# Two engines share the last three output evictions of a sorted-attention and token-mixing kernel

## The chip, the cores and the metric

The kernel runs on one core of a Trainium2 chip. The core has a matrix engine (TensorE, PE in the profile), three engines for elementwise work (VectorE or DVE, ScalarE or ACT, GpSimd or POOL) and SyncE (SP), which here only issues DMA transfers. TensorE writes its results to PSUM, a memory of eight banks; one row of 512 f32 numbers on each of 128 partitions fills one bank. ScalarE and VectorE read PSUM and write SBUF, the working memory, from which DMA takes the output to the chip's main memory (HBM). The metric is the device time of one execution in microseconds (us), of which the median over several runs is compared. A profile is one execution, and its span runs from the first to the last instruction.

## What is computed

Two layers, one behind the other, for 4 batches of 768 positions. The first is attention within blocks of 96 positions, with keys and values mixed over the 8 blocks by a small matrix that is normalised five times. The second mixes positions with weights worked out from the result itself:

```python
# x: the attention's result, (4, 768, 512)
wq = x @ w_q                                   # 512 -> 64
wk = x @ w_k
W_tok = scale * np.einsum('bsd,btd->bst', wq, wk)
mixed = np.einsum('bst,btd->bsd', W_tok, x)
return (np.maximum(mixed, 0.0) @ w_out).astype(np.float32)
```

The change concerns how the last product, `... @ w_out`, leaves the core.

## The kernel before

Everything is tiled by batch (b = 0 to 3), and the stages of neighbouring batches overlap. The order of the work on all engines is written out by hand: ORDER (lines 18 to 48) is a list of short items, each a call of one small function. In an item the first letter is the stage, then come batch and part, then an engine (A ScalarE, D VectorE, G GpSimd, S SyncE) and a PSUM bank. A capital letter is mostly TensorE's work into a bank, and the small letter of the same stage takes the result out of that bank (an eviction). So `O33:0` computes part 3 of the output of batch 3 into bank 0, and `o33:A:0` copies bank 0 to SBUF on ScalarE. Each engine executes its own items in the order of the list. The waits between engines are not written by hand: the tile framework in which the kernel is written puts them in from what each instruction reads and writes.

The positions of a batch are dealt out as 768 = 128 x 6: partition p holds positions 6p to 6p+5, and "row" r of 0 to 5 is the one with remainder r. The last stages of a batch are these:

- H and h (lines 407 to 421): the mixed result, transposed, for two rows at a time, and its relu, which is the eviction to `mixT`. Each call uses two banks. In batch 3 h32 is on VectorE and h30 and h31 are on ScalarE.
- O and o (lines 423 to 432): four accumulating matmuls of 128x512 for each row into one bank, and the copy of that bank into one half of an `ot` tile, which holds two rows in f32. There are four `ot` tiles, used in turn.
- s (lines 434 to 440): the store of a row from `ot` to HBM, issued on SP. In batch 3 each row is a store of its own, 256 KB.

The list ends with batch 3: its rows are computed in the order 5, 4, 0, 3, 2, 1, with the evictions D, A, D, A, A, A. The last three go out of banks 0, 7 and 4, and no later matmul writes these. All eight banks are one tile, `PS` (line 100); `copy` (lines 146 to 150) is `nc.scalar.copy` for the letter A and `nc.vector.tensor_copy` for any other, so that all such copies carry line 148 or 150 in the profile. After the list come a check on GpSimd (lines 443 to 455) of reciprocals that were stored on the way, and a branch to a slow general computation that is not taken here.

Of the kernel before, what the change touches and what calls it, by code (L numbers as in the profile page):

```python
# [42 lines left out]
O12:0 o15:A:3 D30:S H20:6 o12:D:0 H22:2 H21:4 h20:A:6 O13:1 h21:D:4 O20:0 h22:D:2 O23:7 o20:A:0 o13:A:1 J31:2  # L43
o23:D:7 s11:S J30:0 s12:S j31:D:2 O22:7 j30:D:0 d31:D d30:A W31:0 W30:2 o22:A:7 O21:1 w30:D:2 w31:A:0 s21:S
G30:0 o21:D:1 G31:0 s20:S O25:7 g30:A:0 H32:0 o25:A:7 H30:2 H31:4 h32:D:0 h30:A:2 O24:6 O35:0 o24:A:6 h31:A:4
s22:S O34:7 o35:D:0 O30:4 s35:S o34:A:7 O33:0 s34:S o30:D:4 O32:7 s30:S o33:A:0 O31:4 s33:S o32:A:7 s32:S
o31:A:4 s31:S
"""


# [1 line left out]
def kernel(  # L52
# [12 lines left out]
    B, H, S, D = q.shape  # L65
# [9 lines left out]
    DM = moe_w_out.shape[0]  # L75
# [24 lines left out]
    PS = psp.tile([P, 8, 512], FP32, name="ps")  # L100
# [45 lines left out]
    def copy(e, o, i):  # L146
        if e == "A":
            nc.scalar.copy(o, i)  # L148
        else:
            nc.vector.tensor_copy(o, i)  # L150
# [277 lines left out]
    def oslot(b, n):  # L428
        return ot[(b * 3 + n // 2) % NOT]

    def u_o(b, n, e, bank):
        copy(e, oslot(b, n)[:, n % 2, :], PS[:, bank, :])

    def u_s(b, n, e, bank):
        od = out[b].rearrange("(p r) e -> p r e", r=R6)
# [173 lines left out]
    for item in ORDER.split():  # L609
# [5 lines left out]
        b, n = int(name[1]), int(name[2:])  # L615
# [41 lines left out]
```

## Time and profile before

| | us |
|---|---|
| runs before: 99.10, 98.98, 98.49; median | 98.98 |
| profiled execution, its own time | 99.35 |
| span of the profiled execution | 97.5 |
| granted TensorE clock, as a share of full speed | 1.00 |

The page of the profile has the busy time of each engine, the span in 40 slices, the chain of work that ended last (followed back from the last instruction, at each step to what released it) and the costliest groups of instructions. Other views answer questions on the same execution: the chain in order of time, the instructions in order of time, groups with each shape of operand kept apart, who waited for whom, and the DMA transfers. In a row of a group stand the line, the engine, the operation, output and input with their shapes, the count, then busy time in us and the mean of one in ns, and after the next bar the idle time ahead of it with what ended it. In a row of the timeline stand start and duration in us, and in square brackets the idle time before it and what ended it.

### The profile page before, as it was taken

How to read it: one execution, taken by the hardware profiler on the slowest of the kernel's cores; microseconds unless marked ns; L12 is line 12 of the kernel's file. 1: busy time of each engine (PE TensorE's matmuls, PEld its weight loads, DVE VectorE, ACT ScalarE, POOL GpSimd, SP SyncE). 2: the span in 40 equal slices, each digit the busy share in tenths (PEclk: the TensorE clock that was granted, in tenths of full speed). 3: DMA queues.
4: the chain of work that ended last, by engine and by line, in shares of the span. 5: the costliest groups of instructions: out<-in, count | busy, mean ns of one | idle time of the engine just before them, and what ended most of it. 6: DMA issues, size and time to landing. Idle time of an engine off the chain costs nothing.

```text
span 97.5 us, 3326 instructions
## 1 busy us (share of the span) xinstructions
PE 85.6 (88%) x1396; PEld 58.8 (60%) x1406; DVE 66.4 (68%) x133; ACT 70.7 (73%) x102; POOL 30.9 (32%) x50
## 2 busy tenths in 40 slices
PE   4994978959989998989999999999899999999950
PEld 1333567847878576747875687985676555654410
DVE  2677985848995457879876569986596897535300
ACT  5411199987878999979789999899968644549450
POOL 5994009999405860000000077000300380000000
PEclk9999999999999999999999999999999999999999
DMA  0799999999999999999999999889999993691973
GB/s 3 69 199 203 203 205 207 201 203 204 205 217 210 224 246 221 203 206 202 213 248 249 226 198 232 135 176 92 265 424 328 86 245 148 260 383 72 403 309 133
DMA packets 26144, 20.62 MB, mean 211 GB/s; under 512 B 8336, under 2 KB 23440, under 8 KB 26128
## 3 DMA queue, kind: packets, MB, share of 16 engines
q0 software_dynamic: 14064, 10.09, 68.6%
q1 hardware_dynamic: 12064, 10.31, 40.1%
q8 instruction: 11, 0.18, 0.7%
q14 instruction: 5, 0.04, 0.1%
HBM read 20.19 MB, written 6.29 MB: 272 GB/s over the span
## 4 chain that ended last, share of the span: by engine, by line
PE 45%; DMA 32%; POOL 8%; ACT 4%; issue 3%; SPq 2%; DVE 1%; ACTq 0%; DVEq 0%; POOLq 0%
PE ps L144 45%; DMA Vn<-in_v_dram 21%; DMA Qn<-in_q_dram 8%; POOL M L240 5%; DMA VT<-Vs 4%; POOL wqk L209 2%; ACT KT L148 2%; SPq L366 1%; DVE mixT L421 1%; ACT Vs L148 1%; ACT QT L148 1%; POOL Kn L216 1%; POOL wo L211 1%; SPq L302 1%; ACT ot L148 1%
## 5 line engine op out<-in xcount | busy, mean ns | idle before, releaser
L316 ACT ACTIVATE E<-ps 96x960 bf16<-96x960 f32 (+1 forms) x28 | 24.1, 897 | 2.1 <-PE ps L144 1.9
L144 PE MATMUL ps<-wo,mixT 128*128 128x512 bf16 x87 | 22.2, 379 | 0.9 <-issue 0.3
L345 DVE TENSOR_TENSOR X<-ps,Rall 96x896 bf16<-96x896 f32 (+1 forms) x20 | 20.0, 1005 | 0.6
L144 PEld LDWEIGHTS <-mixT 128*128 128x128 bf16 x96 | 8.3, 97 | 9.2 <-issue 0.8
L148 ACT COPY ot<-ps 128x512 f32<-128x512 f32 x17 | 9.9, 586 | 4.8 <-PE ps L144 4.3
L144 PE MATMUL ps<-VT,E 96*128 96x65 bf16 x256 | 10.9, 193 | 0.9 <-DMA VT<-Vs 0.3
L144 PEld LDWEIGHTS <-E 96*128 96x128 bf16 x256 | 9.5, 97 | 3.1 <-issue 2.0
L382 POOL COPY qD<-qkT 64x384 bf16<-64x384 bf16 x4 | 1.9, 500 | 29.1 <-ACT qkT L148 20.0
L148 ACT CAST KT<-ps 128x768 bf16<-128x768 f32 x12 | 9.3, 804 | 1.4 <-PE ps L144 1.0
L240 POOL TENSOR_TENSOR M<-PTR,m_p 128x512 bf16<-128x512 bf16 x6 | 7.8, 1314 | 7.2 <-ACT KT L148 6.1
L144 PEld LDWEIGHTS <-KT 64*128 64x128 bf16 (+1 forms) x288 | 8.3, 97 | 2.7 <-issue 1.2
L150 DVE CAST KT<-ps 128x768 bf16<-128x768 f32 x8 | 7.6, 955 | 2.2 <-PE ps L144 2.1
L144 PE MATMUL ps<-QT,KT 64*128 64x96 bf16 x256 | 9.0, 204 | 0.0
L419 ACT ACTIVATE mixT<-ps 128x1024 bf16<-128x1024 f32 x8 | 8.2, 1025 | 0.6 <-PE ps L144 0.6
L144 PE MATMUL ps<-fil 128*128 128x512 bf16 x21 | 7.4, 526 | 1.4 <-DVE fil L192 1.2
L144 PE MATMUL ps<-M,Kn 128*64 128x128 bf16 x192 | 7.5, 220 | 1.2 <-DMA Kn<-in_k_dram 0.4
L150 DVE COPY ot<-ps 128x512 f32<-128x512 f32 x7 | 4.8, 690 | 4.1 <-PE ps L144 3.8
L144 PEld LDWEIGHTS <-Kn 128*64 128x64 bf16 x192 | 6.4, 109 | 1.9 <-issue 0.8
L148 ACT CAST Vs<-ps 128x1024 bf16<-128x1024 f32 x7 | 6.9, 1017 | 0.8 <-PE ps L144 0.7
L144 PE MATMUL ps<-Vn,M 128*128 128x128 bf16 x72 | 5.5, 219 | 1.5 <-DMA Vn<-in_v_dram 1.3
L421 DVE TENSOR_SCALAR mixT<-ps 128x1024 bf16<-128x1024 f32 x4 | 4.8, 1222 | 2.3 <-PE ps L144 2.2
L340 DVE RECIPROCAL Rall<-ps 96x14 f32<-96x14 f32 (+1 forms) x20 | 4.4, 224 | 2.7 <-PE ps L144 2.7
(80 smaller groups left out, 130.3 us busy)
## 6 DMA issues: line engine op xcount, KB each, us to landing
out_dram<-ot SPq DMA_DIRECT2D x18, 256.0 KB, 2.2
Qn<-in_q_dram POOLq DMA_DIRECT2D x4, 768.0 KB, 22.8
Vn<-in_v_dram POOLq DMA_DIRECT2D x4, 768.0 KB, 18.4
Kn<-in_k_dram POOLq DMA_DIRECT2D x4, 768.0 KB, 17.0
VT<-Vs SPq DMA_DIRECT2D x18, 132.0 KB, 6.4
out_dram<-ot SPq DMA_DIRECT2D x3, 512.0 KB, 4.1
wo<-in_moe_w_out_dram POOLq DMA_DIRECT2D x1, 512.0 KB, 17.0
wqk<-in_moe_w_q_dram POOLq DMA_DIRECT2D x1, 64.0 KB, 14.7
```

What stands on the lines that cost most here:

```text
L144: nc.tensor.matmul(o, w, x, is_transpose=t, start=start, stop=stop, skip_group_check=True)
L148: nc.scalar.copy(o, i)
L150: nc.vector.tensor_copy(o, i)
L209: nc.gpsimd.dma_start(out=wqk[:, :, s, :], in_=w.rearrange("(t p) d -> p t d", p=P))
L211: nc.gpsimd.dma_start(out=wo, in_=moe_w_out.rearrange("(t p) d -> p t d", p=P))
L240: ENG[e].tensor_tensor(out=M[b % 2][:, h0:h0 + hn], in0=src.unsqueeze(2).to_broadcast([P, hn, SP, NB]), in1=m_p.unsqueeze(1).unsqueeze(3). ...
L316: nc.scalar.activation(E[b % 2][:, n, 0:2 * w * BLK].rearrange("p (t a c) -> p a t c", a=2, c=BLK), PS[0:BLK, bank:bank + 2, 0:w * BLK].re ...
L340: nc.vector.reciprocal(Rall[:, b, n, :, 0:w], avps(bank, w)[:, :, :, D])
L345: nc.vector.tensor_mul(xo.rearrange("p (a t d) -> p a t d", a=2, d=D), avps(bank, w)[:, :, :, 0:D], Rall[:, b, n, :, 0:w].unsqueeze(3).to_ ...
L382: nc.gpsimd.tensor_copy(o, i)
L419: nc.scalar.activation(o, i, ACT.Relu)
L421: nc.vector.tensor_relu(o, i)
```

## The change

An item of stage o may now name two engines. The row is then cut into as many pieces of columns as there are letters, and each engine copies its piece: with `AD`, ScalarE columns 0 to 255 and VectorE columns 256 to 511 of the same bank, into the same `ot` tile. The last three evictions of the list, rows 3, 2 and 1 of batch 3, become `AD`; all other items keep one letter and one copy of 512 columns. The matmuls, the banks and the stores stay as they are.

```diff
-s22:S O34:7 o35:D:0 O30:4 s35:S o34:A:7 O33:0 s34:S o30:D:4 O32:7 s30:S o33:A:0 O31:4 s33:S o32:A:7 s32:S
-o31:A:4 s31:S
+s22:S O34:7 o35:D:0 O30:4 s35:S o34:A:7 O33:0 s34:S o30:D:4 O32:7 s30:S o33:AD:0 O31:4 s33:S o32:AD:7 s32:S
+o31:AD:4 s31:S
...
     def u_o(b, n, e, bank):
-        copy(e, oslot(b, n)[:, n % 2, :], PS[:, bank, :])
+        o, w = oslot(b, n)[:, n % 2, :], DM // len(e)
+        for i, x in enumerate(e):
+            copy(x, o[:, i * w:(i + 1) * w], PS[:, bank, i * w:(i + 1) * w])
```

## The prediction

> **What bounds the kernel now.** The page comes first, for the busy shares and for the chain of work that ended last.
>
> ```profile
> span 97.5 us, 3326 instructions
> PE 85.6 (88%) x1396; PEld 58.8 (60%) x1406; DVE 66.4 (68%) x133; ACT 70.7 (73%) x102; POOL 30.9 (32%) x50
> PE 45%; DMA 32%; POOL 8%; ACT 4%; issue 3%; SPq 2%; DVE 1%; ACTq 0%; DVEq 0%; POOLq 0%
> ```
>
> TensorE carries 45% of the chain and loads of the inputs 32%; evictions are a few per cent. But the edit touches three evictions at the very end, so what counts is the last stage. There I read the chain in order of time.
>
> ```profile
> 87.33 1.24 DVE mixT L421
> 88.56 0.05 issue
> 88.61 5.37 PE ps L144 x24
> 93.98 0.02 issue
> 94.00 0.59 ACT ot L148
> ```
>
> From 88.61 on TensorE computes the last six output rows, 24 matmuls without a gap: 5.37/6 = 0.895 us a row at most (the first matmuls overlap the row before). The chain leaves it only when it has finished, and then runs through one eviction, that of row 1. The timeline of the last evictions shows that this is the only one of the six whose length can be seen at the end:
>
> ```profile
> 91.47 0.69 DVE L150 COPY ot<-ps 128x512 f32<-128x512 f32 x1 [1.09 <-PE ps L144]
> 92.27 0.59 ACT L148 COPY ot<-ps 128x512 f32<-128x512 f32 x1 [1.10 <-PE ps L144]
> 93.14 0.59 ACT L148 COPY ot<-ps 128x512 f32<-128x512 f32 x1 [0.28 <-PE ps L144]
> 94.00 0.59 ACT L148 COPY ot<-ps 128x512 f32<-128x512 f32 x1 [0.28 <-PE ps L144]
> ```
>
> These are rows 0, 3, 2 and 1, in that order. ScalarE starts a row every 0.87 us, works 0.59 and then waits 0.28 for TensorE: it is no bottleneck, and VectorE has nothing to do after 91.47 + 0.69 = 92.16. What follows the evictions is SP's queue and the closing of the program:
>
> ```profile
> 92.88 0.33 SPq L440 DMA_DIRECT2D out_dram<-ot  x1
> 93.75 0.33 SPq L440 DMA_DIRECT2D out_dram<-ot  x1
> 94.61 0.33 SPq L440 DMA_DIRECT2D out_dram<-ot  x1
> out_dram<-ot SPq DMA_DIRECT2D x4, 256.0 KB, 2.0
> ```
>
> Each store is issued 0.02 us after its eviction (94.00 + 0.59 = 94.59, issue at 94.61) and lands 2.0 us later (the last line, from the DMA view of 92 us to the end): 96.6. The 0.9 us from there to 97.5 are the barrier at the end. So the last 97.5 - 94.59 = 2.9 us hang rigidly on the end of the last eviction, and the question is when row 1 is out of PSUM.
>
> **The change, part by part.** Three ScalarE copies of 128x512 become three of 128x256, and VectorE gets three of 128x256. The other rows carry one letter, so their width stays DM/1 = 512 and nothing of them moves. The costs come from the groups of instructions with shapes kept apart:
>
> ```profile
> L148 ACT COPY ot<-ps 128x512 f32<-128x512 f32 x17 | 9.9, 586 | 4.8 <-PE ps L144 4.3 <-ACT mixT L419 0.4
> L150 DVE COPY ot<-ps 128x512 f32<-128x512 f32 x7 | 4.8, 690 | 4.1 <-PE ps L144 3.8 <-ACT ot L148 0.3
> L403 ACT ACTIVATE Ab<-ps 128x256 bf16<-128x256 f32 x3 | 1.2, 384 | 1.7 <-PE ps L144 1.7
> L405 DVE TENSOR_SCALAR Ab<-ps 128x256 bf16<-128x256 f32 x1 | 0.4, 416 | 0.0
> L148 ACT COPY wk<-ps 96x256 bf16<-96x256 bf16 x5 | 1.9, 377 | 0.6 <-PE ps L144 0.6
> L150 DVE CAST PTR<-ps 128x256 bf16<-128x256 f32 x1 | 0.4, 414 | 0.0
> ```
>
> No row is the half copy itself (256 columns of f32 out of PSUM into f32), but two of each engine have its length: 0.377 and 0.384 us on ScalarE, 0.414 and 0.416 on VectorE. I take 0.384 and 0.416. Half the columns cost 66% of 0.586 and 60% of 0.690: much of a copy is a fixed part, which is now paid on both engines.
>
> What the trace does not show is how the two halves stand to each other. They lie in one PSUM bank, since a row is the whole of PS[:, bank, :]. In the kernel before, every bank is read by one engine at a time. What it shows is this pair from the timeline, both engines at once:
>
> ```profile
> 87.33 1.23 DVE L421 TENSOR_SCALAR mixT<-ps 128x1024 bf16<-128x1024 f32 x1 [1.69 <-PE ps L144]
> 87.47 1.02 ACT L419 ACTIVATE mixT<-ps 128x1024 bf16<-128x1024 f32 x1
> ```
>
> They read different banks of the one tile PS (0 and 1, 2 and 3) and write different columns of the one tile mixT, side by side. So neither the tile that is read nor the one that is written forces an order; whether a bank does is open. This gives two ends. If the halves run side by side, the slower one counts: 0.416 - 0.586 = -0.170 us, a gain. If VectorE's half has to wait for ScalarE's, both count and the handover between them, for which the nearest rows are an exponential on ScalarE and the reduction on VectorE that waits for it:
>
> ```profile
> 2.81 0.26 ACT L160 ACTIVATE Pm<-Pm 32x64 f32<-32x64 f32 x1 [0.79 <-DVE Pm L172]
> 3.10 0.21 DVE L174 TENSOR_REDUCE tmp<-Pm 32x8 f32<-32x64 f32 x1 [0.32 <-ACT Pm L160]
> ```
>
> The handover is 3.10 - (2.81 + 0.26) = 0.03 us. Then 0.384 + 0.03 + 0.416 - 0.586 = +0.244 us, a loss. I take the serial end. The pair above is concurrent because its banks differ; apart from it every bank in this program passes whole from one engine to the next, with a wait between, and two engines in one bank would be something that this kernel never does. Since waits are put in by the program's dependency tracking and not by hand, a tracker that knows the banks adds this one by itself.
>
> [...]
>
> Now the rest of the path. Row 3: ScalarE 92.27 to 92.65, VectorE 92.68 to 93.10. Row 2: 93.14 to 93.52, then 93.55 to 93.97. Row 1: 94.00 to 94.38, then 94.41 to 94.83, where it was 94.59. VectorE is free at 92.16, 93.10 and 93.97, ahead of each of its halves. Behind its waits stand only its next halves and the drain at its end, so nobody else waits. ScalarE gets freer. TensorE isn't touched: no later row goes into the three banks. If those covers were gone (VectorE's half of row 2 running past 94.41), each 0.1 us would be added to the end one for one.
>
> SP's three stores now wait for two engines. Extra waits appear in the trace as instructions of their own:
>
> ```profile
> L440 SPq EVENT_SEMAPHORE  x13: 17/17/17, 69.4 to 94.1; - x13
> L150 DVEq EVENT_SEMAPHORE  x21: 21/21/2557, 16.1 to 89.7; - x21
> ```
>
> One costs 17 ns on SP (minimum, median and maximum agree) and 21 ns at least on VectorE. ScalarE's half is done 0.45 us before VectorE's, so SP passes that wait early, and VectorE passes TensorE's while ScalarE still reads: both at nothing. In the other order they cost 0.02 each, 0.04 in all. Each of the three stores is issued 0.24 us later, their distance stays 0.87, and their landing stays 2.0 us. SP's queue holds nothing else behind them. VectorE's closing drain moves from 92.16 to 94.83, still before the landing at 96.6 plus 0.24.
>
> Sum: +0.24 us, with ends of 0.377 + 0.03 + 0.414 - 0.586 = +0.235 and 0.244 + 0.04 = +0.28 if serial, and -0.17 if side by side. The profiled execution took 99.35 us, 1.85 more than its span, and would become 99.59. The median of the three runs shown is 98.98 (98.49 to 99.10), 0.37 below the profiled one; on it the forecast is 99.22.
>
> **The rivals.** First, the halves run side by side: the end moves to 94.00 + 0.416 = 94.42, and the median to 98.81. For it speaks that VectorE is idle from 92.16, that the two engines do work at once at 87.5 us, and that the written columns are disjoint. Against it, that no row shows one bank read twice. The point that decides is whether VectorE's copy starts within some 0.05 us of ScalarE's or at its end.
>
> Second, clearly slower: VectorE has to fetch code for instructions that it didn't have. It gets three copies and a few waits, and its list could run over into a further block, fetched only when it is reached. The nearest prices are these, from the DMA view of the whole run:
>
> ```profile
> q14 instruction: 5, 0.04, 0.1%
> Pm<-in_sort_net_dram SPq DMA_DIRECT2D x1, 8.0 KB, 1.6
> ```
>
> Five code packets hold 0.04 MB, 8 KB each, and a transfer of 8 KB took 1.6 us to land. If it stood ahead of the last half it would give 0.24 + 1.6 = 1.84, a median of 100.82. Against it: the chain above has no such wait anywhere near the end (issue is 0.02 us there), so blocks seem to be fetched ahead. It decides only if the boundary falls within the last six instructions or so.
>
> Third, the change doesn't do what it says at the end: a fixed part of the split copy is smaller or larger than in my rows, so that the two orders cancel and nothing is left. For no change the serial pair would have to take 0.586, 0.28 each with the handover; no row of 256 columns above is under 0.377, so this has almost no chance.
>
> **How the numbers follow.** Serial 0.78, side by side 0.13, a code fetch or another stall of over 1 us 0.08, none of these 0.01. The likeliest gives 99.22. For the range, the profiled execution shows that one execution can lie 0.37 above the median; 99.35 + 0.28 = 99.63, so the high end is 99.7. At the low end serial on the fastest run is 98.49 + 0.235 = 98.73, and side by side on the median is 98.81; half of the latter's lower spread (0.17 below the fastest run would be 98.32) takes the low end to 98.5. What is left out is the stall and the low corner of the second case, under 2 in 10.
>
> About 1%, 0.99 us, is what a measurement of this kernel can tell from no change. Serial and side by side both lie within it by a wide margin. Faster by over 1% would need more than the whole eviction of 0.586 to vanish: 0.02, for drift alone. Slower by over 1% holds the stall and drift: 0.10. Within 1%: 0.88.
>
> **What would show it.** In the timeline of the end, six copies of 128x256 stand in place of three of 128x512. Right: VectorE's half of each of the three rows starts about 0.03 us after ScalarE's ends, about 0.41 after it started; the last ends 0.83 us after TensorE's end instead of 0.59; the last store is issued 0.02 us behind it; the time from there to the end of the span stays 2.9 us. The chain's last pieces would be ACT ot 0.38 and DVE ot 0.42. Wrong: halves that start together (the rival, 0.17 less), half copies off 0.38 or 0.42 us (the sizes), a VectorE copy slower than its rows because of ScalarE beside it, a gap before VectorE's copy with both engines done (the code), or a landing of the last store that isn't 2.0 us.

## The result and the profile after

The changed kernel takes 99.34 us (median of 16 runs, 99.24 to 99.85), the kernel before 98.94 (16 runs, 98.49 to 99.17). The ratio is 1.0054, with a 95% interval of 1.0041 to 1.0067: 0.4 to 0.7 us slower. The ratio is worked out from all runs; the two medians alone lie 0.40 us apart, at the low end of it. The forecast was 99.22 us, +0.24.

The profiled execution of the changed kernel took 99.34 us. Two lines of its page, and the last pieces of its chain of waits in order of time (start, length, what):

```profile
span 97.2 us, 3331 instructions
PE 85.7 (88%) x1396; PEld 58.8 (61%) x1406; DVE 67.8 (70%) x136; ACT 70.1 (72%) x102; POOL 30.9 (32%) x50
```

```profile
87.98 5.37 PE ps L144 x24
93.35 0.02 issue
93.37 0.38 ACT ot L148
93.75 0.02 issue
93.77 0.42 DVE ot L150
```

The six rows take TensorE 5.37 us, as before. Behind them the chain now goes through two copies with a gap of 0.02 us between: 0.02 + 0.38 + 0.02 + 0.42 = 0.84 us from TensorE's end to the end of the last copy, where it was 0.02 + 0.59 = 0.61. The timeline of the changed kernel shows the same for all three rows (start, length, in brackets the idle time before and what ended it):

```profile
91.64 0.37 ACT L148 COPY ot<-ps 128x256 f32<-128x256 f32 x1 [1.10 <-PE ps L144]
92.05 0.42 DVE L150 COPY ot<-ps 128x256 f32<-128x256 f32 x1 [0.52 <-ACT ot L148]
92.51 0.37 ACT L148 COPY ot<-ps 128x256 f32<-128x256 f32 x1 [0.49 <-PE ps L144]
92.91 0.42 DVE L150 COPY ot<-ps 128x256 f32<-128x256 f32 x1 [0.44 <-ACT ot L148]
93.37 0.37 ACT L148 COPY ot<-ps 128x256 f32<-128x256 f32 x1 [0.49 <-PE ps L144]
93.77 0.42 DVE L150 COPY ot<-ps 128x256 f32<-128x256 f32 x1 [0.44 <-ACT ot L148]
```

VectorE's idle time ahead of each half ends with ScalarE, never with TensorE. The two engines don't share the row, they take turns. The groups with shapes apart give the means, 373 and 424 ns:

```profile
L150 DVE COPY ot<-ps 128x256 f32<-128x256 f32 x3 | 1.3, 424 | 1.4 <-ACT ot L148 1.4
L148 ACT COPY ot<-ps 128x256 f32<-128x256 f32 x3 | 1.1, 373 | 2.1 <-PE ps L144 2.1
```

The last store and the landing of the last four, from SP's timeline and the DMA view:

```profile
94.23 0.33 SPq L442 DMA_DIRECT2D out_dram<-ot  x1
out_dram<-ot SPq DMA_DIRECT2D x4, 256.0 KB, 2.0
```

One thing in the result isn't in this tail. The profiled execution has 99.34 - 97.2 = 2.1 us outside its span, and that of the kernel before 99.35 - 97.5 = 1.85. The span isn't even longer here: it varies by some tenths from one execution to the next. In these two profiles the difference comes from ahead of the last stage, which starts at 87.98 here and at 88.61 in the kernel before. Over all 16 runs of the changed kernel the time outside the span lies between 2.12 and 2.19 us (the spans are given to a tenth), while the spans lie between 97.1 and 97.7: it varies far less than the span does, and can be compared by itself. It became the second thing to explain.

### The profile page after: what moved, and what is told of

The parts are those of the page before. It is cut to its first block, busy times and chain, and to the rows that moved or that the text cites. A ratio compares the mean times of both kernels' runs of the same rounds, so it can differ in the third digit from the quotient of the medians.

```text
span 97.2 us, 3331 instructions
## 1 busy us (share of the span) xinstructions
PE 85.7 (88%) x1396; PEld 58.8 (61%) x1406; DVE 67.8 (70%) x136; ACT 70.1 (72%) x102; POOL 30.9 (32%) x50
## 4 chain that ended last, share of the span: by engine, by line
PE 52%; DMA 28%; POOL 8%; ACT 3%; issue 2%; DVE 2%; ACTq 0%; DVEq 0%; POOLq 0%
PE ps L144 52%; DMA Vn<-in_v_dram 20%; DMA Qn<-in_q_dram 8%; POOL M L240 5%; POOL wqk L209 2%; DVE mixT L421 1%; ACT Vs L148 1%; ACT QT L148 1%; POOL Kn L216 1%; POOL wo L211 1%; ACT KT L148 1%; DVE ot L150 0%; ACT ot L148 0%; ACT m_p L148 0%; ACTq L148 0%
## 5 line engine op out<-in xcount | busy, mean ns | idle before, releaser
L148 ACT COPY ot<-ps 128x512 f32<-128x512 f32 (+1 forms) x17 | 9.2, 548 | 5.2 <-PE ps L144 4.8
L150 DVE COPY ot<-ps 128x512 f32<-128x512 f32 (+1 forms) x10 | 6.1, 610 | 5.5 <-PE ps L144 3.8
L144 PE MATMUL ps<-XT,wqk 128*128 128x384 bf16 x32 | 6.0, 327 | 0.0
```

The source lines that it names most:

```text
L144: nc.tensor.matmul(o, w, x, is_transpose=t, start=start, stop=stop, skip_group_check=True)
```

## The experiments

In each, `u_o` is that of the change unless the edit says otherwise. They were run in three rounds, and in each the kernel before was timed beside them on the same chip. All results stand together here; "tail" is the time from TensorE's end to the end of the last copy in the profile, by the pieces of the chain or the timeline, and "VectorE's list" counts its instructions in the trace, waits and drains included.

| kernel | ratio to before (95% interval) | outside the span, median us | tail, us | VectorE's list |
|---|---|---|---|---|
| before | 1 | 1.80 to 1.82 | 0.61 | 177 |
| changed | 1.0054 (1.0041 to 1.0067) | 2.15 | 0.84 | 183 |
| changed, again | 1.0062 (1.0040 to 1.0083) | 2.16 | 0.84 | 183 |
| c_single: no row split | 0.9998 (0.9978 to 1.0018) | 1.81 | 0.60 | 177 |
| e_last_only: row 1 split | 1.0042 (1.0020 to 1.0064) | 1.82 | 0.84 | 179 |
| e_first_two: rows 3 and 2 split | 1.0003 (0.9979 to 1.0027) | 1.81 | 0.61 | 181 |
| e_last_DA: row 1, VectorE first | 1.0025 (1.0005 to 1.0045) | 1.80 | 0.85 | 179 |
| e_last_AA: row 1, ScalarE twice | 1.0021 (1.0001 to 1.0042) | 1.81 | 0.67 | 177 |
| e_two_banks | 0.9981 (0.9966 to 0.9995) | 1.80 | 0.39 | 179 |
| e_both_banks | 0.9983 (0.9955 to 1.0012) | 1.81 | 0.39 | 179 |
| e_uneven | 0.9962 (0.9940 to 0.9984) | 1.83 | 0.37 | 179 |
| e_two_stores | 1.0015 (0.9994 to 1.0036) | 1.81 | 0.39 | 179 |
| e_pad6 | 1.0034 (1.0004 to 1.0064) | 2.16 | 0.60 | 183 |
| e_after_less | 1.0020 (0.9991 to 1.0049) | 1.82 | 0.84 | 181 |

**The control.** The function of the change with the old list of items (of the lines that differ, only the items are shown).

```diff
-o33:AD:0
+o33:A:0
...
-o32:AD:7
+o32:A:7
...
-o31:AD:4
+o31:A:4
```

> The function of the change, but with one letter for every row as before, so the instructions are those of the kernel before. Theory (the loss is the serial pair at the last row, and all of it lies between TensorE's end and the end of the span): ratio 1.000, last eviction 0.59 us on ScalarE, 3.57 us from TensorE's end to the end of the span, 1.85 us of the time outside the span. Rival (the 2.15 us outside the span of the changed kernel, against 1.85, belong to the day or the chip and not to the halves): about 2.15 outside the span here too, ratio still 1.000.

The ratio is 0.9998 and the time outside the span 1.81, as for the kernel before beside it (1.80). So the new function costs nothing by itself. This round is not that of the first result, so the control can't tell whether the 2.15 us belonged to that one; for this the changed kernel is run again, below.

**Which row costs.**

```diff
-o33:AD:0
+o33:A:0
...
-o32:AD:7
+o32:A:7
```

> Only the last row, row 1, is split. Theory (tail: only the last eviction is on the path): the same ratio as the whole change, 1.0054, with VectorE's half 0.03 us behind ScalarE's and 3.84 us from TensorE's end to the end of the span. Rival (each split row costs, by its waits or its code): a third of it, ratio 1.002.

```diff
-o31:AD:4
+o31:A:4
```

> Rows 3 and 2 are split, row 1 is one copy on ScalarE as before. Theory (tail): ratio 1.000, within 0.0015, since both rows are out long before row 1; 3.57 us from TensorE's end to the end of the span. Rival (each split row costs): two thirds of the loss, ratio 1.0036.

The chain of the kernel with row 1 alone split ends as that of the whole change:

```profile
93.53 0.02 issue
93.56 0.38 ACT ot L148
93.94 0.02 issue
93.96 0.42 DVE ot L150
```

In the kernel with rows 3 and 2 split, the timeline shows both pairs in turns, and row 1 as one copy, which starts when TensorE is done:

```profile
92.45 0.42 DVE L150 COPY ot<-ps 128x256 f32<-128x256 f32 x1 [0.52 <-ACT ot L148]
92.91 0.37 ACT L148 COPY ot<-ps 128x256 f32<-128x256 f32 x1 [0.49 <-PE ps L144]
93.31 0.42 DVE L150 COPY ot<-ps 128x256 f32<-128x256 f32 x1 [0.44 <-ACT ot L148]
93.77 0.59 ACT L148 COPY ot<-ps 128x512 f32<-128x512 f32 x1 [0.49 <-PE ps L144]
```

Two rows cost nothing (1.0003), one costs all of the tail. That settles it for the theory against a cost of each row, which would have given 1.0036 for the two. My expected 1.0054 for row 1 alone was too much all the same: it has only 1.82 us outside its span, so the tail's 0.24 us, 1.0025, is what it should show. That lies in the measured interval; so does 1.0054, and it is the time outside the span that tells them apart.

**The order of the engines, and one engine for both halves.**

Rows 3 and 2 are whole again from here on (`o33:A:0`, `o32:A:7`), until the time outside the span is taken up; row 1 becomes one of these:

```diff
-o31:AD:4
+o31:DA:4
```

> Only row 1 is split, and VectorE reads first. Theory (the bank passes from one engine to the other whichever comes first): ScalarE starts 0.03 us after VectorE's end, 0.42 + 0.03 + 0.38 = 0.83 us as in the other order, ratio 1.0025 to 1.0045. Rival (it is VectorE's place at the end that costs, for its handover to SP or its end): 0.05 us or more shorter from TensorE's end to the issue of the last store.

```diff
-o31:AD:4
+o31:AA:4
```

> Row 1 is two copies of 256 columns, both on ScalarE, so no engine waits for another. Theory (of the loss of 0.24 us, the fixed part of a second copy is about 0.18 and the handover and VectorE's slower columns the rest): 2 x 0.375 = 0.75 us if the copies stand one after the other, about 0.65 if they overlap as two copies of 512 columns on ScalarE did in the profile of the kernel before (0.1 us), so 0.07 to 0.16 more than one copy; ratio 1.0007 to 1.002. Rival (the handover between engines is the larger part): under 0.62 us, ratio 1.000.

With VectorE first, ScalarE waits for it in turn; the chain's last pieces:

```profile
93.51 0.02 issue
93.53 0.44 DVE ot L150
93.97 0.02 issue
93.99 0.37 ACT ot L148
```

That is 0.85 us and a ratio of 1.0025: the order doesn't matter, and VectorE's place at the end has no cost of its own. With both halves on ScalarE the group of the two copies shows what a second copy costs without a second engine:

```profile
L148 ACT COPY ot<-ps 128x256 f32<-128x256 f32 x2 | 0.6, 376 | 0.3 <-PE ps L144 0.3
94.07 0.65 ACT L148 COPY ot<-ps 128x256 f32<-128x256 f32 x2 [0.28 <-PE ps L144]
```

Each takes 376 ns, but together they are busy for 0.65 us and not 0.75: on one engine the second begins before the first has ended. That is 0.06 to 0.07 us more than the single copy of 0.586. The other 0.17 us of the loss belong to the two engines: the overlap of 0.10 that is lost, 0.02 to 0.03 for the handover, and 0.05 for VectorE's longer copy (424 against 376 ns). The ratio, 1.0021, has an interval (1.0001 to 1.0042) too wide to tell 0.07 us from 0.24, so these sizes rest on the profile.

**Two banks.** Row 1 is computed as two halves of columns in banks 4 and 5 (free by then).

```diff
     def u_O(b, n, bank):
-        for t in range(PT):
-            mm(PS[:, bank, :], mixT[b % NMIX][:, t // 2, t % 2, n, :], wo[:, t, :],
-               start=(t == 0), stop=(t == PT - 1))
+        k = 2 if (b, n) == (B - 1, 1) else 1
+        w = DM // k
+        for h in range(k):
+            for t in range(PT):
+                mm(PS[:, bank + h, 0:w], mixT[b % NMIX][:, t // 2, t % 2, n, :], wo[:, t, h * w:(h + 1) * w],
+                   start=(t == 0), stop=(t == PT - 1))
...
-            copy(x, o[:, i * w:(i + 1) * w], PS[:, bank, i * w:(i + 1) * w])
+            copy(x, o[:, i * w:(i + 1) * w], PS[:, bank + i, 0:w])
...
-o31:AD:4
+o31:DA:4
```

> Rows 3 and 2 are one copy each on ScalarE as before. Row 1 is computed in two halves of 256 columns, eight matmuls of 128x256 in place of four of 128x512, into two banks (4 and 5); VectorE takes the first half while TensorE computes the second, ScalarE takes the second. Theory (the shared bank makes the halves wait for each other, nothing else): VectorE's half ends before ScalarE's, which ends 0.38 to 0.40 us after TensorE's end in place of 0.61, ratio about 0.998, if the eight matmuls take no longer than the four. Rival (the second engine or the second wait itself costs at the end): no gain, ratio 1.000 or above. If the eight matmuls are slower, TensorE's last row takes over 0.87 us and the gain goes there.

The first half leaves while TensorE computes the second, as its timeline shows:

```profile
92.83 0.58 ACT L148 COPY ot<-ps 128x512 f32<-128x512 f32 x1 [0.28 <-PE ps L144]
93.27 0.42 DVE L150 COPY ot<-ps 128x256 f32<-128x256 f32 x1 [1.42 <-PE ps L144]
93.71 0.37 ACT L148 COPY ot<-ps 128x256 f32<-128x256 f32 x1 [0.29 <-PE ps L144]
```

Both halves wait for TensorE now and not for each other. The eight matmuls take at most 0.02 us longer than the four: ScalarE starts row 1's second half at 93.71, 0.88 us after row 2 at 92.83, where the distance was 0.86 to 0.87. The tail is 0.39 us, the ratio 0.9981 (0.9966 to 0.9995), a small gain as expected. But here VectorE is done (93.69) before ScalarE starts (93.71), so the two don't meet, and the shared output tile could still be what kept them apart. The next kernel takes the matmuls of the halves in turn, so that both come due nearly together:

```diff
-        for h in range(k):
-            for t in range(PT):
+        for t in range(PT):
+            for h in range(k):
```

> Row 1 in two halves of 256 columns in two banks as in the earlier run, but with the matmuls of the halves taken in turn, so that both halves are ready at nearly the same time; rows 3 and 2 as before. Both engines write the same row of the same tile as in the change; only the bank is not shared. Theory (the shared bank is what makes the second half wait): VectorE and ScalarE copy at the same time, overlapping by 0.3 us or more, both done 0.40 us after TensorE's end, ratio 0.998. Rival (the shared output tile, or the second engine as such, makes it wait): one copy starts when the other ends, 0.83 us less 0.1 after TensorE's end, ratio 1.001 or above.

```profile
93.98 0.42 DVE L150 COPY ot<-ps 128x256 f32<-128x256 f32 x1 [1.75 <-PE ps L144]
94.08 0.37 ACT L148 COPY ot<-ps 128x256 f32<-128x256 f32 x1 [0.29 <-PE ps L144]
```

From 94.08 to 94.40 both copies run, 0.32 us side by side, neither longer than alone, into the same row of the same `ot` tile. So neither that tile nor the second engine is the cause of the turns. What is gone is the shared bank, and with it the shared matmuls: each half now has four of its own. The ratio, 0.9983 (0.9955 to 1.0012), can't show so small a gain; this rests on the profile.

The packed traces also tell which semaphore an instruction waits for. In the changed kernel VectorE's three half copies wait for the one that ScalarE's copies raise (number 111); in these two kernels its copy of row 1 waits for the one that the matmuls raise (109). So the turns are a wait in the program, put in by the framework, and not something that the engines come to while they run. Two halves that are computed apart but lie in one bank were not run, so whether the framework goes by the bank or by the matmuls that both halves come from is not shown.

The 0.32 us side by side are two engines that read two banks at once. What two reads of one bank at once would do, no run here shows.

**A shorter last piece, and a cut store.** The cut of row 1 is moved to 384 and 128 columns, VectorE's piece first (shown against the first kernel with two banks):

```diff
+    def cuts(b, n):
+        return [(0, 384), (384, DM)] if (b, n) == (B - 1, 1) else [(0, DM)]
...
-        for h in range(k):
+        for h, (c0, c1) in enumerate(cuts(b, n)):
             for t in range(PT):
-                mm(PS[:, bank + h, 0:w], mixT[b % NMIX][:, t // 2, t % 2, n, :], wo[:, t, h * w:(h + 1) * w],
+                mm(PS[:, bank + h, 0:c1 - c0], mixT[b % NMIX][:, t // 2, t % 2, n, :], wo[:, t, c0:c1],
                    start=(t == 0), stop=(t == PT - 1))
...
-        o, w = oslot(b, n)[:, n % 2, :], DM // len(e)
+        o = oslot(b, n)[:, n % 2, :]
         for i, x in enumerate(e):
-            copy(x, o[:, i * w:(i + 1) * w], PS[:, bank + i, 0:w])
+            c0, c1 = cuts(b, n)[i]
+            copy(x, o[:, c0:c1], PS[:, bank + i, 0:c1 - c0])
```

> Row 1 in two banks, first 384 columns for VectorE, then 128 for ScalarE, computed in this order; rows 3 and 2 as before. Theory (what is left at the end is one copy, of a fixed part and a part by columns): VectorE's copy of 384 columns takes 0.56 us from the end of its matmuls, so it ends about 0.3 us after TensorE's end, since TensorE's last four matmuls of 128 columns take 0.22 to 0.25 us; ScalarE's of 128 columns takes 0.27; 0.30 to 0.35 us after TensorE's end in place of 0.61, ratio 0.9965 to 0.998. Rival (small matmuls don't run faster in proportion): TensorE's last row takes 0.1 us longer and the ratio stays at 0.998.

```profile
92.16 1.47 PE L144 MATMUL ps<-wo,mixT 128*128 128x512 bf16 x10
93.44 0.56 DVE L150 COPY ot<-ps 128x384 f32<-128x384 f32 x1 [1.63 <-PE ps L144]
93.67 0.27 ACT L148 COPY ot<-ps 128x128 f32<-128x128 f32 x1 [0.29 <-PE ps L144]
```

The first row holds TensorE's last matmuls, put together under the form of the first; they end at 92.16 + 1.47 = 93.63. Both copies have the expected lengths, but VectorE's piece, at 94.00, is now the last, 0.37 us after TensorE's end, a little later than expected: this cut is too uneven. This kernel is the fastest of the study, 0.9962 (0.9940 to 0.9984), against 0.9981 for the even cut; the intervals overlap, so that it beats the kernel before is shown, and that it beats the even cut is not.

Then the store of row 1 is cut in two as well, one store for each half, on top of the even cut:

```diff
+        if (b, n) == (B - 1, 1):
+            for h in range(2):
+                c = slice(h * DM // 2, (h + 1) * DM // 2)
+                ENG[e].dma_start(out=od[:, n, c], in_=oslot(b, n)[:, n % 2, c])
+            return
```

> Row 1 in two banks as in the run before of that name, and besides its store cut into two of 128 KB, the first issued when VectorE's half is out. Theory (the last 128 KB land sooner than 256 KB, by their share of the bandwidth: 0.3 us at the 350 to 400 GB/s of the windows): ratio 0.995, landing of the last store 1.7 us after its issue. Rival (the landing is a fixed time and not a matter of bytes, and the second issue of 0.33 us on SP is in the way): landing 2.0 us, ratio 0.998 as with one store, or worse.

The ratio is 1.0015 (0.9994 to 1.0036), not the expected 0.995: the gain of the two banks is given back. SP's timeline, the DMA view and SP's closing waits say where:

```profile
94.61 0.35 SPq L447 DMA_DIRECT2D out_dram<-ot  x1
95.07 0.39 SPq L447 DMA_DIRECT2D out_dram<-ot  x1
out_dram<-ot SPq DMA_DIRECT2D x2, 128.0 KB, 1.8
L662 SPq EVENT_SEMAPHORE  x3: 28/28/28, 96.8 to 97.0; - x3
L662 SPq EVENT_SEMAPHORE  x6: 27/28/28, 97.0 to 97.3; - x6
```

The half store does land sooner, 1.8 us after its issue and not 2.0, so bytes count a little. But ScalarE's copy had ended at 94.41 + 0.37 = 94.78, and SP issued its store only at 95.07, since it was still busy with the first until 94.61 + 0.35 = 94.96 and had a wait of 17 ns behind it, at 95.0: 0.29 us lost. And SP's waits for all stores at the end of the program come in a fixed order, not in that of the landings: in the packed trace they go up by the number of the semaphore, and that of the last store, 108, is the third. The last store landed at 96.8, and the seven waits behind it ran to 97.3 (the one at 97.0 stands in both lines) although all that they waited for was there: 0.5 us more. With one store, in the kernel of the even cut, the wait for the last landing is also the last of them, at 96.1 with the drain right behind it:

```profile
L657 SPq EVENT_SEMAPHORE  x4: 28/28/28, 95.3 to 96.1; - x4
L657 SPq DRAIN  x1: 13/13/13, 96.2 to 96.2; - x1
```

The rival was right in that the second issue is in the way, and the order of the waits, which neither had seen, costs more.

**What lies outside the span.** First the changed kernel once more.

> The changed kernel once more, beside the kernel before on the same chip. It took 2.15 us outside its span in all its 16 executions, where the kernel before and its other variants took 1.80. Theory (that 0.35 us belongs to the session or chip and not to the change): 1.80 outside here, a span 0.25 us longer than that of the kernel before, ratio about 1.0025 and at most 1.004. Rival (it belongs to the three split rows together, by the length or placing of the code): 2.15 outside again, ratio 1.0055 to 1.006.

It has 2.16 us outside the span, and the kernel before beside it 1.82. So it belongs to the kernel and not to a round or a chip; my theory fell here. Rows 3 and 2 split give 1.81, and row 1 split 1.82, but all three 2.16: a step, not a price for each row. What grows steadily with the rows is VectorE's list, two instructions for each (a copy and a wait): 177, 179, 181, 183. Two kernels test that. The first has six added instructions and no split row:

```diff
+    pad = sb.tile([P, 2], BF16, name="pad")
...
+    for _ in range(6):
+        nc.vector.memset(pad, 0.0)
     off = guard()
```

> Every row is evicted as before. At the end of VectorE's list stand six added memsets of 128x2 on a tile that nothing reads, behind its last eviction, where it would be idle: six instructions, as many as the change adds to VectorE in the profile (177 to 183 with its waits). Theory (the changed kernel's 2.15 us outside the span, against 1.80, come from the length of VectorE's list, which passes some limit between 181 and 183): 2.15 us outside the span, the span as before, ratio about 1.0035. Rival (they come from the split evictions themselves, or the waits between the engines): 1.80 us outside, ratio 1.000.

The second has all three rows split, and two instructions less on VectorE:

```diff
             for t in KT:
-                nc.vector.memset(t[:, :, S:S + PAD], 0.0)
+                nc.scalar.copy(t[:, :, S:S + PAD], fil[:, 0:NP * PAD].rearrange("p (n x) -> p n x", n=NP))
```

> The whole change, but the two memsets of the keys' padding on VectorE at the start are two copies of zeros on ScalarE, which waits there anyway: VectorE's list has 181 instructions in place of 183, ScalarE's two or so more. Theory (length of VectorE's list): 1.80 us outside the span, the tail still 0.25 us longer than before, ratio 1.0025. Rival (the three split evictions themselves): 2.15 us outside, ratio 1.0055.

The timeline of the first shows the six memsets where VectorE is idle, and row 1 as before:

```profile
91.61 0.70 DVE L625 MEMSET pad<- 128x1 uint32 x6
93.50 0.58 ACT L149 COPY ot<-ps 128x512 f32<-128x512 f32 x1 [0.28 <-PE ps L145]
```

Yet the kernel has 2.16 us outside its span (2.10 to 2.20 over its 12 runs), with a ratio of 1.0034. The second is back at 1.82 (1.76 to 1.85), with the pairs still in turns. So in these kernels the step comes with VectorE's list between 181 and 183 instructions and not with the split. It does not show as code that is fetched inside the span: the pages of the kernel before, of the changed one and of both test kernels count the same packets of code,

```profile
q8 instruction: 11, 0.18, 0.7%
q14 instruction: 5, 0.04, 0.1%
```

and where q14 has a sixth, in the changed kernel run again and in that with rows 3 and 2 split, the one has 2.16 us outside the span and the other 1.81. Why a list of 183 instructions goes with 0.34 us more outside the span stays open, since the profile shows nothing there.

## Why the prediction was right, and where it fell short

- **What bounds the end.** Right: only row 1 is on the path. Splitting rows 3 and 2 costs nothing, splitting row 1 alone costs the whole tail.
- **The serial end of the bounds.** Right, and the wait is in the program, as was said: VectorE's halves wait for the semaphore that ScalarE's copies raise (111) and start 0.02 us after their end. With a bank for each half the two copies ran 0.32 us side by side. That banks decide this, as the prediction says of the pair at 87.33, was the author's inference: no run shows whether it is the bank or the shared matmuls that the wait goes by.
- **The sizes.** 0.384 and 0.416 were taken, 0.373 and 0.424 measured; the handover was put at 0.03 and is 0.02 in the chain. The tail's growth of 0.24 came out as 0.84 - 0.61 = 0.23; ScalarE's half was put 0.011 too long and VectorE's 0.008 too short, so the two nearly cancel.
- **The waits on SP.** Nearly right: the store is issued at 94.23, 0.04 us after VectorE's end at 94.19, where 0.02 was forecast. The landing stayed at 2.0. From the last copy's end to the end of the span it is 97.2 - 94.19 = 3.0 us, where 2.9 was to stay: no more than the later issue and the rounding of the spans.
- **The step that failed.** "The profiled execution took 99.35 us, 1.85 more than its span, and would become 99.59." The time outside the span was carried over as a constant, and it grew to 2.15. The sum of both, 0.24 + 0.34 = 0.58 us, is a ratio of 1.006, inside both intervals of the changed kernel (1.0041 to 1.0067, and 1.0040 to 1.0083). The forecast of 99.22 was low by that term. The base of three runs, 98.98, lies 0.04 above the median of all 16, which hid a little of it. Between the two medians, 0.40 apart, less than 0.58 is seen, since the spans vary by some tenths.
- **The range.** It held 99.34, but not for its own reason: the room up to 99.7 was left for the scatter of a single execution, 0.37 us, and none of it for a change outside the span, which took 0.34. That part is luck. At the low end, half of the 0.49 us between 98.81 and 98.32 leads to 98.57 and not to 98.5; nothing came of it.
- **The second rival.** It pointed at VectorE's longer list, with which the miss comes, but saw a code fetch of 1.6 us in a visible gap ahead of the last half. There is no gap and no further packet of code in the span; the price is 0.34 us and lies behind or ahead of everything that the profile shows. Whether code is the reason, and whether it is fetched only when it is reached, is not shown.
- **The first rival**, halves side by side, is what the kernel does that computes the halves in two banks in turn: the tail falls to 0.39 us.
- **The third rival**, nothing left to see, did not come: the pair takes 0.82 us where one copy took 0.59.

## What to carry to other kernels

In these kernels two engines shared the eviction of a row only when its halves lay in two PSUM banks (0.32 us side by side); in one bank they took turns, and half the columns took 373 of 586 ns on ScalarE and 424 of 690 on VectorE, so that with the handover of 0.02 the tail grew from 0.61 to 0.84 us where a gain was meant. What gained at the end of this kernel is worth a trial in others: the last product cut over two banks, so that only a piece was left to copy when TensorE was done (a tail of 0.37 to 0.39 us, a ratio of 0.996 to 0.998), and one store for it (1.0015 with two). Compare the time outside the span too: six memsets on an idle engine went with 2.16 us there, where the kernel before had 1.82.

## What the runs showed that I had not expected

- With VectorE's list at 183 instructions in the trace 0.34 us more lay outside the span, in two programs measured three times in all (2.15 to 2.16 us); at 181 or fewer the others have 1.80 to 1.83 us.
- SP's closing waits follow the order of its semaphores. A last store that stood early in it left the other waits to run behind its landing, 0.5 us.
- Two copies on ScalarE, one after the other out of one bank, took 0.65 us together at 0.376 each.
